# The first DFT stage of a long convolution: mirrored rows, one 8 KB run per row, order by hand

## The chip, the cores and the metric

The kernel runs on one core of a Trainium2 chip. The metric is the device time in microseconds (us). Three runs of the kernel before took 1265.47, 1269.49 and 1283.69 us, with a median of 1269.49.

A core has TensorE (PE), which multiplies a stationary operand (loaded first; the profile lists the weight load as PEld) with a moving one into PSUM, VectorE (DVE), ScalarE (ACT) and GpSimd (POOL), which work element by element, and SyncE (SP), which here only issues DMAs. DMAs are issued from SP's and ACT's queues and run on 16 DMA engines. Each engine works through its own instructions in order and waits for others by semaphores.

## What is computed

Inputs are x and v of 4 batches × 12800 positions × 128 channels, and a filter that comes from a small network.

```python
h_mlp = np.maximum(pos_emb @ w1, 0.0) @ w2
h_filt = h_mlp * np.exp(-0.01 * pos)[:, None]
u = x * v
y = causal_convolution(u, h_filt)        # by FFT of length 2 * 12800 in the reference
x1 = x * y
gate = sigmoid(sum_k conv_w[k] * x1 shifted by 4 - k positions)    # 5 taps
out = (gate * (x1 @ w_val)) @ w_out
```

All of it is float32. The gate's weights are 200 times larger than drawn, so small errors in x1 show in the output.

## The kernel before, in words

The 12800 positions are two halves (j) of 6400 = 100 × 64; a position is j·6400 + n1·64 + n2 with n1 below 100 and n2 below 64. The convolution is done in the frequency domain by a two-step DFT with odd frequencies 4·k1 + 1, which needs cosine and sine parts only.

**First stage** (span 0 to about 404 us). Partitions are n1. `chunks` lists 64 chunks, each one j and two n2. `fetch` loads x and v of a chunk for all four batches, `prep` multiplies them on DVE (u_t, line 257), and splits the product in a rounded part u_hi (ACT, line 258) and a rest u_lo (POOL, line 259), because the matmul is done in the fast float32r form. In `signal` each of four pieces (two batches, cosine or sine, 512 columns) is the sum of three matmuls: rounded table × u_hi, table's rest × u_hi, rounded table × u_lo (line 282). PSUM is copied by ACT (cosine, line 285) and DVE (sine, line 287) into st, and two DMAs store st into the DRAM tensor a_u, the cosine's on ACT's queue and the sine's on SP's. `_Split` (line 102) issues every such DMA as two, rows 0 to 95 and rows 96 to 99.

Beside it `filt` computes the filter's spectrum: transposes of pos_emb (tp, posT), the network's first layer (gp, g_sb), the 100-point DFT of the 64 hidden columns (ap, copied into ag), and then, for each k1, a 64-point DFT with a table fk that ACT and DVE build (lines 232 and 233) and PE applies (line 235). `signal` and `filt` are generators; a list of costs interleaves their steps, and a scheduler orders the recorded instructions by a timeline. Three weights come as 64-bit words and are narrowed on DVE by `_narrow`, at the ninth chunk.

**Second stage** (about 404 to 860 us). Fifty pairs of k1: a pair's rows of a_u are loaded (128 partitions of 4 KB, line 359), transformed over n2 (z_ps, line 341), multiplied with the filter's spectrum on DVE, combined on POOL, transformed back (c_ps, line 369, whose two row halves of 64 are two row tiles of the array), copied by ACT (line 376), and stored in c_y by ACT's queue in runs of 2 KB. The order is written by hand.

**Third stage** (about 860 us to the end). Rows of c_y (4 KB onto 100 partitions) and of x are loaded, the last 100-point transform, the product with x, the five taps, the gate and the two projections follow.

Buffers: the pool `ld` has six buffers of 128 × 2048 floats, which all stages share; u_t, u_hi, u_lo have two, st three.

## Time and profile before

| | |
|---|---|
| median of three runs | 1269.49 us |
| span of the profiled execution | 1273.6 us (its own time is not listed apart; the span stands for it) |
| PE, DVE busy over the span | 1144.7 us (90%), 1018.0 us (80%) |
| POOL, ACT busy over the span | 862.4 us (68%), 628.3 us (49%) |
| DMA over the span | 332.95 MB, 261 GB/s on average |
| first stage | last store issued at 403.7 us, first read of a_u at 408.2 us |

Busy times are those of one profiled execution. A group's row gives its source line, engine, operation, what it writes and reads, the shape and the count; then the busy time in us, the mean of one in ns, and the engine's idle time just before these instructions with what ended it. DMA share is the mean busy share of the 16 DMA engines. Shares over the whole span mix three stages with different limits, so the first stage has to be read by itself.

### The profile page before, as it was taken

To read this page: it belongs to the slowest core of one execution; us is meant where nothing else is said; L and a number is where in the kernel's file an instruction comes from. 1 tells how busy PE (TensorE), PEld (TensorE's weight loads), DVE (VectorE), ACT (ScalarE), POOL (GpSimd) and SP (SyncE) were. 2 spreads that over 40 slices of the span, in tenths; PEclk is the share of its full clock that TensorE was granted. 3 is DMA by queue.
4 is the path that set the end of the run, shared out by engine and by line. 5 is a ranking of instruction groups with operands and counts; after the bars stand their busy time and mean duration, and the time that the engine had idled before them with its cause. 6 is when DMAs were issued, how large, how long until landed. Compare 5 with 4: busy or idle time off the path is not lost. (4 is left out here: it accounts for less than half of the span.)

```text
span 1273.6 us, 16726 instructions
## 1 busy us (share of the span) xinstructions
PE 1144.7 (90%) x5500; PEld 570.2 (45%) x5500; DVE 1018.0 (80%) x1130; ACT 628.3 (49%) x1064; POOL 862.4 (68%) x346
## 2 busy tenths in 40 slices
PE   4878999978867889999999999988899999999986
PEld 3657776656544223333333333334344444444432
DVE  5956233797744999999999999951999999999997
ACT  3334454677633223333333333323576677667663
POOL 3334233434543669999999999962788988987980
PEclk9979899989977999999999999988999999999999
DMA  9999778889996667777787778539999989999942
GB/s 240 304 306 302 231 231 268 269 250 299 297 303 220 260 231 261 269 278 281 283 296 276 277 275 297 215 132 264 247 286 283 290 264 286 286 272 281 291 150 103
DMA packets 152255, 332.95 MB, mean 261 GB/s; under 512 B 12447, under 2 KB 64715, under 8 KB 150635
## 3 DMA queue, kind: packets, MB, share of 16 engines
q1 hardware_dynamic: 104256, 226.13, 58.8%
q10 hardware_dynamic: 47914, 105.76, 22.9%
q8 instruction: 45, 0.74, 0.2%
q14 instruction: 40, 0.32, 0.1%
HBM read 200.77 MB, written 131.07 MB: 261 GB/s over the span
## 5 line engine op out<-in xcount | busy, mean ns | idle before, releaser
L530 POOL TENSOR_TENSOR ext<-yr,xr 128x400 f32<-128x400 f32 x120 | 298.1, 2486 | 48.9 <-DVE yr L528 46.5
L259 POOL TENSOR_TENSOR u_lo<-u_t,u_hi 100x1024 fp32r<-100x1024 f32 x64 | 159.0, 2488 | 241.3 <-ACT u_hi L258 223.0
L545 DVE SCALAR_TENSOR_TENSOR gt<-ext,cw,gt 128x1600 f32<-128x1600 f32 x128 | 242.6, 1895 | 1.8 <-ACT gt L542 1.8
L376 ACT COPY c_sb<-c_ps 128x1024 f32<-128x1024 f32 x100 | 101.4, 1014 | 279.2 <-PE c_ps L369 279.2
L341 PE MATMUL z_ps<-ld 128*64 128x512 f32 x800 | 194.7, 606 | 7.9 <-DMA ld<-a_u 6.8
L428 POOL TENSOR_TENSOR va<-va,vb 128x1024 f32<-128x1024 f32 x50 | 156.4, 3127 | 36.6 <-DVE vb L346 36.5
L282 PE MATMUL fp<-u_hi,fwd_hi 100*100 100x512 f32 x256 | 118.7, 464 | 55.8 <-ACT st L285 21.8
L287 DVE COPY st<-fp 100x512 f32<-100x512 f32 x128 | 85.2, 685 | 74.2 <-PE fp L282 58.2
L503 PE MATMUL sd<-ld,inv 100*64 100x512 f32 x512 | 129.8, 611 | 10.6 <-DMA ld<-c_y 9.1
L346 DVE TENSOR_TENSOR vb<-z_ps,h_sb 128x2048 f32<-128x2048 f32 x50 | 114.5, 2289 | 23.8 <-ACT c_sb L376 23.6
L429 POOL TENSOR_TENSOR vc<-vc,vd 128x1024 f32<-128x1024 f32 x50 | 118.3, 2365 | 21.8 <-DVE vd L346 17.1
L564 PE MATMUL o_ps<-gd,wout 128*128 128x400 f32 x256 | 112.0, 519 | 18.3 <-DVE gd L559 10.7
L257 DVE TENSOR_TENSOR u_t<-ld 100x1024 f32<-100x1024 f32 x64 | 87.4, 1366 | 50.8 <-POOL u_lo L259 42.0
L346 DVE TENSOR_TENSOR va<-z_ps,h_sb 128x2048 f32<-128x2048 f32 x50 | 114.0, 2280 | 11.3 <-PE z_ps L341 11.3
L510 ACT COPY sd_sb<-sd 128x512 f32<-128x512 f32 x128 | 76.2, 596 | 90.4 <-PE sd L503 66.9
L430 POOL TENSOR_TENSOR va<-va,vb 128x1024 f32<-128x1024 f32 x50 | 118.4, 2368 | 0.0
L369 PE MATMUL c_ps<-vc,ld 64*128 64x512 f32 x400 | 100.7, 622 | 14.6 <-DVE vc L419 14.5
L282 PE MATMUL fp<-u_hi,fwd_lo 100*100 100x512 f32 x256 | 110.7, 432 | 0.0
L285 ACT COPY st<-fp 100x512 f32<-100x512 f32 x128 | 71.1, 594 | 76.0 <-PE fp L282 46.7
L554 PE MATMUL v_ps<-ext,wval 128*128 128x400 f32 x256 | 107.1, 500 | 0.0
L341 PEld LDWEIGHTS z_ps<-ld 128*64 128x64 f32 x800 | 54.4, 138 | 113.3 <-issue 85.6
L258 ACT CAST u_hi<-u_t 100x1024 fp32r<-100x1024 f32 x64 | 68.2, 1067 | 73.1 <-PE fp L282 40.9
(78 smaller groups left out, 1951.4 us busy)
## 6 DMA issues: line engine op xcount, KB each, us to landing
c_y<-c_sb ACTq DMA_DIRECT2D x100, 512.0 KB
ld<-a_u SPq DMA_DIRECT2D x49, 1024.0 KB
ld<-c_y SPq DMA_DIRECT2D x128, 384.0 KB
xr<-in_xt_dram SPq DMA_DIRECT2D x32, 800.0 KB
out_dram<-o_sb ACTq DMA_DIRECT2D x32, 800.0 KB
ld<-in_x_dram SPq DMA_DIRECT2D x64, 384.0 KB
ld<-in_v_dram SPq DMA_DIRECT2D x64, 384.0 KB
a_u<-st ACTq DMA_DIRECT2D x64, 384.0 KB
```

Of the source, the lines that this page charges most:

```text
L259: nc.gpsimd.tensor_tensor(lo, u_t, hi.bitcast(F32), op=ALU.subtract)
L282: nc.tensor.matmul(out=fp, lhsT=w[:, c], rhs=d[:, b:b + 2], start=(k == 0), stop=(k == 2))
L341: nc.tensor.matmul(out=z[half[h]], lhsT=wk[:, h, half[c]], rhs=a2[:, h, j], start=True, stop=True)
L346: nc.vector.tensor_tensor(out, z.rearrange("p (b d) -> p b d", d=D).unsqueeze(1).to_broadcast([128, n, B, D]), h_sb.unsqueeze(2).to_broadc ...
L428: nc.gpsimd.tensor_tensor(va[:, 0:2], va[:, 0:2], vb[:, 0:2], op=ALU.add)
L429: nc.gpsimd.tensor_tensor(vc, vc, vd, op=ALU.add)
L430: nc.gpsimd.tensor_tensor(va[:, 2:4], va[:, 2:4], vb[:, 2:4], op=ALU.add)
L503: nc.tensor.matmul(out=sd[c * N2:(c + 1) * N2], lhsT=inv[:, c], rhs=ct[c][:, r * B * D:(r + 1) * B * D], start=True, stop=True)
L530: nc.gpsimd.tensor_tensor(e[:, r0 + r], yr, xr, op=ALU.mult)
L545: nc.vector.scalar_tensor_tensor(gt, rows(t, k), cw[:, k:k + 1], gt, op0=ALU.mult, op1=ALU.add)
L554: nc.tensor.matmul(out=v_ps, lhsT=wval, rhs=rows(t)[:, r * ROW:(r + 1) * ROW], start=True, stop=True)
L564: nc.tensor.matmul(out=o_ps, lhsT=wout, rhs=gd, start=True, stop=True)
```

## The change

The transform over n1 is taken about the middle of the 100 rows, half a sample off. Row q and its mirror image 99 − q then have cosines that are equal and sines that are opposite, so the sum and the difference of the two rows carry everything, and 50 rows are contracted instead of 100.

- The host lays x and v out anew: for each n2 one row per (half of the batches h, pair q), with x and v, both j, the row and its mirror, two batches and 128 channels side by side: 2048 floats, 8 KB. The hundred rows (h, q) stand on partitions 14 to 113, so that h = 0 ends at partition 63 and h = 1 starts at 64.
- The 64 chunks are now the 64 values of n2, each with both j. `product` multiplies x and v on DVE (line 278). `folded` makes sums and differences on POOL, two instructions of 512 columns (line 286). `spectra` applies two tables (cos + sin to the sums, cos − sin to the differences) in full float32: per table two matmuls, one per h, on partitions 0 to 63 and 64 to 127 (line 296). The split into rounded part and rest is gone. The copies to st have 1024 columns each (lines 299 and 301).
- `store` writes a row's 2048 floats as one run; a_u is [k1, n2, 2, j, b, d] now. All of it goes by SP's queue. The second stage's table is recomputed for the two new parts, and its load takes them in the order (n2, part).
- Five of the six `ld` buffers hold chunks in rotation, fetched five ahead; the sixth holds pos_emb in two halves. The unused partitions of the five are cleared by ten memsets at the start (lines 313 and 314). u has two buffers, f three, st four.
- `filt` does the same work in a pipelined order (a step's matmuls are issued with the next step), g_sb is stored with n2 innermost, and the steps return their own cost; the loop over n2 is under a manual schedule. `_narrow` stands after n2 = 40, 46 and 52.

```diff
-        def prep(i):
-            x_t, v_t = ahead.pop(0)
-            u_t = p1.tile([N1, B, P1C * D], F32, name="u_t", bufs=2)
-            hi = p1.tile([N1, B, P1C * D], F32R, name="u_hi", bufs=2)
-            lo = p1.tile([N1, B, P1C * D], F32R, name="u_lo", bufs=2)
-            nc.vector.tensor_tensor(u_t, x_t, v_t, op=ALU.mult)
-            nc.scalar.copy(out=hi, in_=u_t)
-            nc.gpsimd.tensor_tensor(lo, u_t, hi.bitcast(F32), op=ALU.subtract)
-            return hi, lo
...
-                for b in range(0, B, 2):
-                    for c in range(2):
-                        fp = ps1.tile([N1, 2, P1C, D], F32, name="fp", bufs=4)
-                        for k, (w, d) in enumerate(((fwd_hi, hi), (fwd_lo, hi), (fwd_hi, lo))):
-                            nc.tensor.matmul(out=fp, lhsT=w[:, c], rhs=d[:, b:b + 2], start=(k == 0), stop=(k == 2))
...
+        def fetch(n):
+            t = held[n % XB]
+            sync_s.dma_start(out=t[P0:P0 + N1], in_=xv[n].rearrange("h q w j l b d -> (h q) (w j l b d)"))
+            return t.rearrange("p (w e) -> p w e", w=2)
+
+        def product(n):
+            t = fetched.pop(n)
+            u = p1.tile([128, J, 2, XE], F32, name="u", bufs=2)
+            nc.vector.tensor_tensor(
+                u.rearrange("p j l e -> p (j l e)"), t[:, 0], t[:, 1], op=ALU.mult)
+            us[n] = u
+
+        def folded(n):
+            u = us.pop(n)
+            f = p1.tile([128, 2, J, XE], F32, name="f", bufs=3)
+            for c, op in ((0, ALU.add), (1, ALU.subtract)):
+                nc.gpsimd.tensor_tensor(f[:, c], u[:, :, 0], u[:, :, 1], op=op)
+            folds[n] = f
+
+        def spectra(n):
+            f = folds.pop(n)
+            st = p1.tile([128, 2, J, B, D], F32, name="st", bufs=4)
+            for c in range(2):
+                fp = ps1.tile([128, 2, J, XE], F32, name="fp", bufs=2)
+                for h in range(2):
+                    r = slice(h * NH, (h + 1) * NH)
+                    nc.tensor.matmul(out=fp[:, h], lhsT=fold[r, c], rhs=f[r, c], start=True, stop=True)
+                o = st[:, c].rearrange("k j (h b) d -> k h j (b d)", h=2)
+                if c == 0:
+                    nc.scalar.copy(out=o, in_=fp)
+                else:
+                    nc.vector.tensor_copy(out=o, in_=fp)
+            done[n] = st
+
+        def store(n):
+            st = done.pop(n).rearrange("k c j b d -> k (c j b d)")
+            dst = a_u[:, n].rearrange("k c j b d -> k (c j b d)")
+            sync_s.dma_start(out=dst, in_=st[P0:P0 + N1])
+
+        fetched, us, folds, done = {}, {}, {}, {}
+        AHEAD1 = 5
+        with tc.manual_schedule():
+            for t in held:
+                nc.vector.memset(t[0:32], 0.0)
+                nc.vector.memset(t[96:128], 0.0)
+            fetched[0] = fetch(0)
+            fil = filt()
+            n_fil, spent = 16 * 1.3 + 0.7 + 16 * 0.9 + 16 * 1.5 + 25 * 1.9 + 0.5, 0.0
+            for n in range(1, AHEAD1):
+                fetched[n] = fetch(n)
+            product(0)
+            folded(0)
+            product(1)
+            for n in range(N2):
+                if n + AHEAD1 < N2:
+                    fetched[n + AHEAD1] = fetch(n + AHEAD1)
+                if n + 1 < N2:
+                    folded(n + 1)
+                if n + 2 < N2:
+                    product(n + 2)
+                spectra(n)
+                while spent < n_fil * (n + 1) / (N2 - 2):
+                    step = next(fil, None)
...
+                if n:
+                    store(n - 1)
+                if n == 40:
                     _narrow(nc, p1, wval, w_val)
+                if n == 46:
                     _narrow(nc, p1, wout, w_out)
+                if n == 52:
                     _narrow(nc, p1, cw, conv_w.rearrange("k d -> d k"))
...
-                    in_=a_u[2 * p + i:2 * p + i + step].rearrange("k c n j b d -> (c n) k (j b d)"))
+                    in_=a_u[2 * p + i:2 * p + i + step].rearrange("k n c j b d -> (n c) k (j b d)"))
```

Where the instructions moved stands in the prediction, at the two places it rests on: DMA issues on SP in the middle of the stage, and DVE where the tables fk are built. Names there: a_u and st are the spectra on their way to DRAM, ld a chunk of x and v, in_x, in_v and in_xv the inputs before and after, u_t and u the products, fk the filter's tables, raw, top and tmp the words of `_narrow`.

More of the change, by code (lines that the diff above doesn't have):

```diff
@@ L27 @@
 KG = 8
-P1C = 2
+NF, NH = N1 // 2, 64
+P0 = NH - NF
 R = 4
@@ L60, in _tables @@
     win = np.transpose(win, (1, 0, 2))
-    tabs = {"fwd": fwd, "inv": inv, "w": w, "dft": dft, "tw": tw, "win": win, "ident": np.eye(128)}
+    tabs = {"fwd": fwd, "fold": fold, "inv": inv, "w": w, "dft": dft, "tw": tw, "win": win, "ident": np.eye(128)}
     return {k: np.ascontiguousarray(a, dtype=np.float32) for k, a in tabs.items()}
@@ L148, in tile_longconv_gate @@
     cw = const.tile([D, KC], F32, name="cw")
+    nc.scalar.dma_start(out=fold, in_=t_fold)
     nc.scalar.dma_start(out=fwd, in_=t_fwd)
@@ L164, in load @@
         return ld.tile([128, 2048], F32, name="ld")
-    def split(src, name):
-        hi = const.tile(list(src.shape), F32R, name=name + "_hi")
-        lo = const.tile(list(src.shape), F32R, name=name + "_lo")
-        nc.vector.tensor_copy(out=hi, in_=src)
-        nc.vector.tensor_tensor(lo, src, hi.bitcast(F32), op=ALU.subtract)
-        return hi, lo
-    fwd_hi, fwd_lo = split(fwd, "fwd")
     ag_pool = tc.tile_pool(name="ag", bufs=1)
@@ L232, in filt @@
                     nc.scalar.activation(fk[:, i], dft[:, 1], AF.Copy, scale=tw[:, 1, k1:k1 + 1])
+                for i in range(4):
+                    k1 = k0 + i
                     nc.vector.scalar_tensor_tensor(
                         fk[:, i], dft[:, 0], tw[:, 0, k1:k1 + 1], fk[:, i], op0=ALU.mult, op1=ALU.add)
-                    nc.tensor.matmul(
-                        out=gz[:, i], lhsT=ag[:, k1].rearrange("p j e -> p (j e)"), rhs=fk[:, i], start=True, stop=True)
-                nc.scalar.copy(out=ag[:, k0:k0 + 4].rearrange("p k j e -> p k (j e)"), in_=gz)
@@ L238, in filt @@
-                yield
-        xv = x.rearrange("b (j a n) d -> j a b n d", j=J, a=N1)
-        vv = v.rearrange("b (j a n) d -> j a b n d", j=J, a=N1)
-        chunks = [(j, n0) for j in range(J) for n0 in range(0, N2, P1C)]
-        def fetch(i):
-            j, n0 = chunks[i]
-            ns = slice(n0, n0 + P1C)
-            t = load()[:N1].rearrange("a (w b e) -> a w b e", w=2, b=B)
-            for w, src in enumerate((xv, vv)):
-                sync_s.dma_start(out=t[:, w], in_=src[j][:, :, ns].rearrange("a b n d -> a b (n d)"))
-            return t[:, 0], t[:, 1]
@@ L264, in signal, with after @@
-        def signal():
-            ready = [prep(0)]
-            for i, (j, n0) in enumerate(chunks):
-                if i == 8:
+                if after:
+                    after()
+                def after(k0=k0, fk=fk):
+                    gz = ps1.tile([128, 4, 2 * N2], F32, name="gp", bufs=1)
+                    for i in range(4):
+                        nc.tensor.matmul(
+                            out=gz[:, i], lhsT=ag[:, k0 + i].rearrange("p j e -> p (j e)"), rhs=fk[:, i],
+                            start=True, stop=True)
+                    nc.scalar.copy(out=ag[:, k0:k0 + 4].rearrange("p k j e -> p k (j e)"), in_=gz)
@@ L289, in signal @@
-                for c in range(2):
-                    (scalar_s if c == 0 else sync_s).dma_start(
-                        out=a_u[:, c, ns, j].rearrange("k n b d -> k n (b d)"),
-                        in_=st[:, c].rearrange("k n b d -> k n (b d)"))
-        FS = 0.9
-        sig, fil = signal(), filt()
-        n_sig = len(chunks) * B // 2
-        cost = [0.7, 0.9] * (J * N2 // 8) + [0.8] * (FO // 4) + [1.6] * (FO // 4) + [0.9] * (N1 // 4)
-        spent, steps = 0.0, iter(cost)
-        for i in range(n_sig):
-            next(sig, None)
-            while spent < sum(cost) and spent * n_sig * FS <= (i + 1) * sum(cost):
-                next(fil, None)
-                spent += next(steps, sum(cost))
@@ L305, in tile_longconv_gate @@
-        for _ in sig:
-            pass
-        for _ in fil:
-            pass
+            for _ in fil:
+                pass
+            store(N2 - 1)
     with tc.tile_pool(name="p2", bufs=1) as p2, tc.tile_pool(name="ps2", bufs=1, space=PSUM) as ps2:
```

101 lines of the change are left out of this document (59 added, 42 removed).

## The prediction

> **What bounds the kernel now.** The kernel has three stages, and the change touches the first alone. I began with the busy time by stretch of the span, to see where the first stage ends and what is full in it. The columns are the stretch, its length, then busy us (and instructions) of PE, PE weight load, DVE, ACT and POOL, the granted clock, the mean share of the 16 DMA engines and GB/s.
>
> ```profile
> core 0: us, PE busy (x) PEld busy (x) DVE busy (x) ACT busy (x) POOL busy (x), PEclk, DMA share, GB/s
> 0.00:404.00 404.00, 333.51 (x1930) 244.39 (x1932) 246.15 (x367) 202.93 (x350) 159.21 (x68) 0.92 0.89 271
> 20.00:120.00 100.00, 80.90 (x454) 60.48 (x454) 77.56 (x124) 34.79 (x50) 36.96 (x15) 0.93 0.99 302
> 120.00:400.00 280.00, 243.93 (x1453) 178.50 (x1454) 159.68 (x230) 161.24 (x288) 116.20 (x47) 0.90 0.86 264
> 410.00:420.00 10.00, 7.30 (x27) 3.41 (x28) 5.03 (x3) 1.14 (x3) 0.40 (x1) 0.74 1.01 393
> 500.00:600.00 100.00, 100.00 (x476) 34.34 (x474) 93.43 (x60) 37.53 (x59) 93.92 (x36) 1.00 0.79 279
> 860.00:900.00 40.00, 32.29 (x144) 15.18 (x142) 13.31 (x29) 15.13 (x33) 14.67 (x12) 0.91 1.00 268
> ```
>
> Two things are nearly full in the first 404 us: PE at 333.5 us (83%) and the DMA engines at 0.89. The stage moves 404 × 271 = 109.5 MB. Dividing GB/s by share gives what the DMA engines would move at full share: 302/0.99 = 305 and 264/0.86 = 307 in this stage, 279/0.79 = 353 in the second, 268 at the start of the third, and 393/1.01 = 389 while the second stage fetches its first rows. So with PE taken away altogether the stage would still need 109.5/306 = 358 us of DMA.
>
> Next the groups of instructions of the stage, the list of waits from 20 to 400 us, and the handover to the second stage on the timeline.
>
> ```profile
> L282 PE MATMUL fp<-u_hi,fwd_hi 100*100 100x512 f32 x256 | 118.7, 464 | 55.8 <-ACT st L285 21.8 <-ACT u_hi L258 20.2 <-DVE st L287 12.6
> L257 DVE TENSOR_TENSOR u_t<-ld 100x1024 f32<-100x1024 f32 x64 | 87.4, 1366 | 50.8 <-POOL u_lo L259 42.0 <-DMA ld<-in_x_dram 3.1 <-DMA a_u<-st 2.8
> L287 DVE COPY st<-fp 100x512 f32<-100x512 f32 x128 | 85.2, 685 | 74.2 <-PE fp L282 58.2 <-DMA a_u<-st 15.9
> L258 ACT CAST u_hi<-u_t 100x1024 fp32r<-100x1024 f32 x64 | 68.2, 1067 | 73.1 <-PE fp L282 40.9 <-DVE u_t L257 9.2 <-DMA a_u<-st 7.5
> L259 POOL TENSOR_TENSOR u_lo<-u_t,u_hi 100x1024 fp32r<-100x1024 f32 x64 | 159.0, 2488 | 241.3 <-ACT u_hi L258 223.0 <-PE gp L235 18.2
> L233 DVE SCALAR_TENSOR_TENSOR fk<-dft,tw,fk 128x128 f32<-128x128 f32 x100 | 51.6, 565 | 10.8 <-ACT fk L232 10.7
> DVE st L287 <- PE fp L282: 58.0, 44, 4.9
> ACT st L285 <- PE fp L282: 44.5, 30, 5.3
> ACT st L285 <- DMA a_u<-st: 18.5, 8, 5.6
> 403.70 1.47 SPq L102 DMA_DIRECT2D a_u<-st  x2
> 408.22 2.36 SPq L359 DMA_DIRECT2D ld<-a_u  x5
> 411.73 1.09 PE L341 MATMUL z_ps<-ld 128*64 128x512 f32 x1 [6.83 <-DMA ld<-a_u]
> ```
>
> DVE and ACT wait for PE (58 and 44.5 us), and PE in turn for them: the engines hand a chunk round in a ring, and the 11% of idle DMA comes from it. The stage ends when the last store has landed (issue at 403.7, first read at 408.2), and the second stage starts 8 us behind the last store's issue. That handover stays as it is, so what the stage gains or loses the kernel gains or loses.
>
> **The change part by part: TensorE.** The three split matmuls per chunk, 768 in all, go, and 256 of 64 rows by 512 columns in two row tiles come. The second stage has the same form; the first row is the busy time of the old matmuls alone in the stage.
>
> ```profile
> 0.00:404.00 404.00, 226.17 (x768) 133.02 (x768) 0.92 0.89 271
> L369 PE MATMUL c_ps<-vc,ld 64*128 64x512 f32 x400 | 100.7, 622 | 14.6 <-DVE vc L419 14.5
> L376 ACT COPY c_sb<-c_ps 128x1024 f32<-128x1024 f32 x100 | 101.4, 1014 | 279.2 <-PE c_ps L369 279.2
> ```
>
> They cost 100.7/400 = 0.252 us apiece, so 64 us in place of 226 us, and PE falls from 333 to about 171 us. If the two row tiles do not overlap, the bound is 256 × 0.622 = 159 us and 266 us in all, still far below the DMA time. PE stops being a bound either way.
>
> **ACT, DVE and POOL.** ACT loses the cast (68 us) and copies 64 times 1024 elements at 1.014 us (65 us for 71). DVE keeps its 64 products at 1.37 us and its copies (64 × 2 × 0.685 = 88 us at most). POOL trades 64 subtractions of 1024 elements for 128 sums and differences of 512. No row has POOL at 512, so the bounds are half of 2.488 us and all of it. I take half, 1.24, since its rows of 1024 scale with the elements, and POOL stays near 159 us. New on DVE are ten memsets of 32x2048 at the very start. The sizes nearest to them stand at the start of the timeline, with the first fetch of now and the wait for the first table:
>
> ```profile
> 0.83 0.17 DVE L151 MEMSET w1bd<- 128x128 f32 x1 [0.83 <-PEq L645]
> 1.00 0.27 DVE L152 MEMSET w2bd<- 128x256 f32 x1
> 0.74 0.88 SPq L102 DMA_DIRECT2D ld<-in_x_dram  x2
> 4.45 0.32 DVE L169 CAST fwd_hi<-fwd 100x300 fp32r<-100x300 f32 x1 [3.18 <-DMA fwd<-in_tab_fwd_dram]
> ```
>
> 128 columns more cost 0.10 us, so 2048 columns cost 0.27 + 14 × 0.10 = 1.67 us and ten cost 17 us. Each fetch waits for the two memsets of its buffer. The first leaves at about 4.6 us where now it leaves at 0.74, the fifth at 18, and the sixth waits for the first product at 19. Five fetches are 4.1 MB, 12 us of transfer, so the DMA engines lose about 6 us there. DVE as a whole comes to 246 + 17 = 263 us, so it does not bound the stage as a total.
>
> **The transfers** are the term that decides. The bytes stay, to 0.1 MB, but a row's run becomes 8 KB each way. Here are DMA issues on SP in the middle of the stage, before the change (ld is the chunk's x and v, st its spectra; the bracket names what an issue waits for).
>
> ```order
> L102 DMA a_u_63<-st_2375 96x2x512 [waits DMAHW7_49,DVE_49]
> L102 DMA a_u_63<-st_2375 4x2x512 [waits DMAHW0_49]
> L102 DMA ld_2847<-in_x_dram 96x4x256 [waits DMAHW1_49,DVE_49]
> L102 DMA ld_2847<-in_x_dram 4x4x256 [waits DMAHW2_49]
> L102 DMA ld_2847<-in_v_dram 96x4x256 [waits DMAHW3_49]
> ```
>
> The same queue after the change:
>
> ```order
> L113 DMA a_u_63<-st_1567 96x2048 [waits DMAHW2_49,DVE_49,Activation_49]
> L113 DMA a_u_63<-st_1567 4x2048 [waits DMAHW3_49]
> L113 DMA ld_101<-in_xv_dram 96x2048 [waits DMAHW4_49]
> L113 DMA ld_101<-in_xv_dram 4x2048 [waits DMAHW5_49]
> L113 DMA a_u_63<-st_1600 96x2048 [waits DMAHW6_49,DVE_49,Activation_49]
> L113 DMA a_u_63<-st_1600 4x2048 [waits DMAHW7_49]
> ```
>
> A load row was four runs of 1 KB (256 floats) and a store row two of 2 KB; both are now one of 8 KB (2048 floats). All stores moved onto SP, ahead of the next fetch, where half of them were ACT's. With eight semaphores in turn and two issues per transfer, about four transfers of 0.82 MB are in flight, so a store that waits for its copies holds up the fetch behind it, but three transfers (7 us) cover that.
>
> No row shows 8 KB on 100 partitions in both directions. Above stand 389 (4 KB reads onto 128 partitions) and 353 (4 KB reads with 2 KB writes, 128 partitions); below stand 306 (this stage, short runs, 100 partitions) and 268 (the third stage's 4 KB reads onto 100 partitions, with its x rows). The partitions and the mix of reads and writes are those of 306, the run length points to 353, and I take the middle, 330: 109.5/330 = 332 us. [...]
>
> **What is late next.** In the last part of the stage DVE's order changes. Here it stands at the tables fk, before the change (u_t and u are products, st copies of the spectra).
>
> ```order
> L233 SCALAR_TENSOR_TENSOR fk<-dft,tw,fk 128x128 x3
> L287 COPY st<-fp 100x2x2x128
> L233 SCALAR_TENSOR_TENSOR fk<-dft,tw,fk 128x128 x5
> L257 TENSOR_TENSOR u_t<-ld 100x1024
> L287 COPY st<-fp 100x2x2x128 x2
> ```
>
> And after it, at the second of the three weights that are narrowed there:
>
> ```order
> L278 TENSOR_TENSOR u<-ld 128x1024
> L301 COPY st<-fp 128x2x2x256
> L252 SCALAR_TENSOR_TENSOR fk<-dft,tw,fk 128x128 x4
> L86 TENSOR_SCALAR top<-raw 128x128
> L87 TENSOR_SCALAR tmp<-raw 128x128
> L88 TENSOR_TENSOR top<-top,tmp 128x128
> ```
>
> The narrowing moved from the stage's beginning into the fk stretch, between four fk and the next chunk's product, which follows its last row. Its first instruction waits for a load issued just ahead of it; the only row of such a wait is the 3.2 us for the table fwd. With some dozen small instructions behind it I charge 5 us for each of the three, 15 us, between nothing (the transfers in flight cover it) and 25. At the end the last chunk's product, fold, matmuls and copy (1.2 + 2.5 + 1.0 + 1.4 us) leave the DMA engines half idle: 5 us.
>
> The sum: 332 + 6 + 15 + 5 = 358 us where 404 stood, 46 us less. The profiled span is 1273.6 us, so 1227.6, and since it is 4.1 us over the median of the runs (1269.49), the forecast is 1223.5 us.
>
> **The rivals.** *Full speed transfers* (0.15): at 353 the stage takes 310 + 26 = 336 us, 68 less, and the time is 1201.5. At 389 it would be 1173, but DVE's 263 us and the waits round it keep it from going so low; I stop at 320 us, 1185. For it speaks the one run per row, against it the 100 partitions.
>
> *Run length is worth nothing* (0.17): 306 stays, 358 + 26 = 384, 20 less, 1249.5. For it: the quotient is the same, 305 and 307, in a full and in a less full stretch, so it looks like a property of the traffic.
>
> *DVE and POOL shut each other out* (0.10):
>
> ```profile
> L257 DVE TENSOR_TENSOR u_t<-ld x64: 1208/1216/3415, 7.9 to 394.8; 100x1024 f32<-100x1024 f32 x64
> L233 DVE SCALAR_TENSOR_TENSOR fk<-dft,tw,fk x100: 334/341/2546, 15.6 to 333.1; 128x128 f32<-128x128 f32 x100
> L287 DVE COPY st<-fp x128: 673/684/702, 23.1 to 403.0; 100x512 f32<-100x512 f32 x128
> ```
>
> Minimum, median, maximum: products and fk are at times longer by one POOL subtraction (2.2 us of 2.5), copies from PSUM never. In the fk stretch (25 steps over 28 chunks) a chunk has 2.5 us on POOL, 1.2 for the product and 0.9 × 4 × 0.34 = 1.2 for fk, which exclude each other: 4.9 us, just the DMA time of a chunk (1.64 MB / 330 = 5.0). If each chunk also waits out one POOL instruction (1.24), it adds 28 × 1.2 = 34 us: 392, 12 less, 1257.5.
>
> *The four odd rows pace the queue* (0.06): every transfer is split into 96 and 4 rows. If four of the 16 engines always had 7 rows against a mean of 6.25, the transfers would take 332 × 7/6.25 = 372, the stage 398, and the time 1263.5. Against it: with the same split the mean share reached 0.99, where four pacing engines allow 0.89. [...]
>
> *100 partitions throttle long runs* (0.07), the slower side: at 268, the third stage's price, the transfers take 409, the stage 435, 31 more, and the time is 1300.5. It is slower from below 109.5/(404 − 26) = 290, and by over 2% below 272. For it: that row is the only one with long reads onto 100 partitions. Against it: there nearly all packets are reads, here half.
>
> **How the numbers follow.** The forecast keeps 0.45; its own range, with 318 to 345 GB/s and 8 to 22 us for the narrowing, is 1201 to 1242. Two per cent, about what can be told from no change, is 1244 and 1295. Below 1244 lie the forecast (0.43), full speed (0.15), a third of the 306 case (0.06) and a little of the DVE case (0.02): 0.66. Above 1295 lies most of the last rival, 0.06; 0.28 remains. The range 1188 to 1262 leaves out that rival, half of the odd-row case and the ends of the first.
>
> **What would show it.** The stage's last store at about 358 us with GB/s over share near 330 confirms the main term; a share well under 0.9 in the middle would say that an engine bounds it instead. PE busy near 171 us, POOL's fold near 1.24 us, the first product at 19 us, and DVE idle at the three narrowings test the rest. Wrong would be a quotient at 306 or below, or an fk stretch over 5.5 us per chunk.

## The result and the profile after

The changed kernel takes 1253.76 us (median; 1249.01 to 1274.54) where the kernel before, run beside it, takes 1269.53 us (1255.66 to 1285.80). The ratio is 0.9925 with a 95% interval of 0.9899 to 0.9951: faster by 0.5 to 1.0%, less than the 2% that was named as the bound. The forecast was 1223.5 us, and only about a third of the expected 46 us has come. The time lies inside the range 1188 to 1262, but the range reached to within 8 us of the time before; a time below 1244 had been given 0.66, one within 2% of the time before, as it came, 0.28.

The busy time by stretch of the first stage (columns as in the prediction: stretch, length, PE, PE weight load, DVE, ACT, POOL, granted clock, DMA share, GB/s) shows where it stays:

```profile
core 0: us, PE busy (x) PEld busy (x) DVE busy (x) ACT busy (x) POOL busy (x), PEclk, DMA share, GB/s
0.00:389.00 389.00, 260.18 (x1672) 142.98 (x1672) 251.78 (x311) 133.24 (x222) 166.25 (x132) 0.86 0.88 281
0.00:60.00 60.00, 26.23 (x136) 15.66 (x136) 44.06 (x41) 7.36 (x7) 21.07 (x20) 0.94 0.81 222
60.00:260.00 200.00, 149.08 (x1208) 87.10 (x1208) 107.20 (x116) 70.98 (x102) 90.12 (x71) 0.86 0.97 314
260.00:360.00 100.00, 62.52 (x234) 30.05 (x234) 74.14 (x122) 39.42 (x85) 39.88 (x30) 0.75 0.78 249
360.00:389.00 29.00, 22.35 (x97) 10.16 (x96) 26.38 (x34) 15.49 (x31) 15.19 (x12) 1.00 0.83 288
```

The stage moves 389 × 281 = 109.3 MB, as before. In its middle no engine is near full, and the DMA share is 0.97 with 314 GB/s; at the start and in the fk stretch the share is lower and so is the rate. Price the lost bytes at 314 GB/s. From 0 to 60 us 13.3 MB are moved, worth 42 us, so 18 are lost. From 260 to 360 us 24.9 MB, worth 79: 21 lost. From 360 on 8.4 MB, worth 27: 2 lost. With 109.3 / 314 = 348 us for the bytes that makes 389.

The groups of instructions of the stage (line, engine, operation, shapes, count, then busy us, mean ns, then idle time before them with what ended it):

```profile
L296 PE MATMUL fp<-f,fold 64*128 64x512 f32 x512 | 160.3, 738 | 101.9 <-POOL f L286 47.6 <-ACT st L299 43.1 <-DVE st L301 10.9
L286 POOL TENSOR_TENSOR f<-u 128x512 f32<-128x512 f32 x128 | 166.1, 1320 | 219.1 <-DVE u L278 198.5 <-PE ap L239 9.7 <-PE fp L296 5.8
L278 DVE TENSOR_TENSOR u<-ld 128x1024 f32<-128x1024 f32 x64 | 80.6, 1261 | 47.3 <-DMA ld<-in_xv_dram 44.7 <-POOL f L286 2.4
L299 ACT COPY st<-fp 128x1024 f32<-128x1024 f32 x64 | 64.8, 1012 | 211.5 <-PE fp L296 110.2 <-DMA a_u<-st 97.1 <-PE gp L260 3.7
L313 DVE MEMSET ld<- 32x2048 f32 x5 | 8.8, 1765 | 2.3 <-issue 2.3
L86 DVE TENSOR_SCALAR top<-raw 128x128 int32<-128x128 int32 (+1 forms) x3 | 0.6, 209 | 34.1 <-DMA raw<-in_moe_w_val_dram 16.6 <-DMA raw<-in_moe_conv_w_dram 9.4 <-DMA raw<-in_moe_w_out_dram 8.1
```

DVE waits 44.7 us for loads before its products, and ACT 97.1 us for a store to free the tile of spectra: both ends of the pipe wait for transfers, which the kernel before did not show to this degree (18.5 us for ACT's copy, 3.1 us for the product). The last row is the second loss: DVE stands 34.1 us before the first instruction of the three narrowings. The timeline shows the end of the memsets with the first product, the narrowing's first wait, and the handover to the second stage:

```profile
19.52 1.76 DVE L313 MEMSET ld<- 32x2048 f32 x1 [0.48 <-issue]
21.75 1.76 DVE L314 MEMSET ld<- 32x2048 f32 x1 [0.47 <-issue]
23.54 2.36 DVE L278 TENSOR_TENSOR u<-ld 128x1024 f32<-128x1024 f32 x2
...
259.24 0.33 ACTq L80 DMA_DIRECT2D raw<-in_moe_w_val_dram  x1
259.74 1.01 ACT L299 COPY st<-fp 128x1024 f32<-128x1024 f32 x1 [9.36 <-DMA a_u<-st]
267.37 0.23 DVE L86 TENSOR_SCALAR top<-raw 128x128 int32<-128x128 int32 x1 [16.65 <-DMA raw<-in_moe_w_val_dram]
...
272.08 5.97 POOL L286 TENSOR_TENSOR f<-u 128x512 f32<-128x512 f32 x4 [22.30 <-DVE u L278]
...
389.23 0.68 SPq L113 DMA_DIRECT2D a_u<-st  x2
393.73 2.42 SPq L394 DMA_DIRECT2D ld<-a_u  x5
397.03 1.94 PE L376 MATMUL z_ps<-ld 128*64 128x512 f32 x2 [6.63 <-DMA ld<-a_u]
```

The last store is issued at 389.2 us (403.7 before, 358 forecast) and the second stage's first matmul of z_ps starts at 397.0 us (411.7 before): 14.7 us gained. This start, the first number behind the three durations in the row below, is the measure of the stage in all experiments, each read from one profiled execution; a time given without a ratio is that of a single run. The second number is the start of the last such matmul, the end of the second stage.

```profile
L376 PE MATMUL z_ps<-ld x800: 592/592/1116, 397.0 to 817.5; 128*64 128x512 f32 x160
```

### The profile page after: what moved, and what is told of

Its sections match the earlier page's. It is cut to its first block, busy times and chain, and to the rows that moved or that the text cites. A ratio compares the mean times of both kernels' runs of the same rounds, so it can differ in the third digit from the quotient of the medians.

```text
span 1251.4 us, 15855 instructions
## 1 busy us (share of the span) xinstructions
PE 1073.3 (86%) x5244; PEld 470.7 (38%) x5244; DVE 1014.8 (81%) x1074; ACT 558.7 (45%) x936; POOL 874.0 (70%) x410
## 5 line engine op out<-in xcount | busy, mean ns | idle before, releaser
L286 POOL TENSOR_TENSOR f<-u 128x512 f32<-128x512 f32 x128 | 166.1, 1320 | 219.1 <-DVE u L278 198.5
L296 PE MATMUL fp<-f,fold 64*128 64x512 f32 x512 | 160.3, 738 | 101.9 <-POOL f L286 47.6
L463 POOL TENSOR_TENSOR va<-va,vb 128x1024 f32<-128x1024 f32 x50 | 159.5, 3190 | 38.8 <-DVE vb L381 19.5
L299 ACT COPY st<-fp 128x1024 f32<-128x1024 f32 x64 | 64.8, 1012 | 211.5 <-PE fp L296 110.2
L381 DVE TENSOR_TENSOR vb<-z_ps,h_sb 128x2048 f32<-128x2048 f32 x50 | 114.6, 2291 | 25.2 <-ACT c_sb L411 24.9
L599 PE MATMUL o_ps<-gd,wout 128*128 128x400 f32 x256 | 112.3, 520 | 17.9 <-DVE gd L594 10.4
L381 DVE TENSOR_TENSOR va<-z_ps,h_sb 128x2048 f32<-128x2048 f32 x50 | 114.1, 2282 | 11.6 <-PE z_ps L376 11.1
L278 DVE TENSOR_TENSOR u<-ld 128x1024 f32<-128x1024 f32 x64 | 80.6, 1261 | 47.3 <-DMA ld<-in_xv_dram 44.7
L465 POOL TENSOR_TENSOR va<-va,vb 128x1024 f32<-128x1024 f32 x50 | 118.6, 2371 | 0.0
L296 PEld LDWEIGHTS fp<-f,fold 64*128 64x128 f32 x512 | 53.2, 217 | 159.2 <-POOL f L286 81.9
L301 DVE COPY st<-fp 128x1024 f32<-128x1024 f32 x64 | 78.1, 1220 | 31.7 <-DMA a_u<-st 20.4
L404 PE MATMUL c_ps<-va,ld 64*128 64x512 f32 x400 | 99.4, 615 | 0.1
```

The costliest lines, as they stand in the source:

```text
L286: nc.gpsimd.tensor_tensor(f[:, c], u[:, :, 0], u[:, :, 1], op=op)
L296: nc.tensor.matmul(out=fp[:, h], lhsT=fold[r, c], rhs=f[r, c], start=True, stop=True)
L381: nc.vector.tensor_tensor(out, z.rearrange("p (b d) -> p b d", d=D).unsqueeze(1).to_broadcast([128, n, B, D]), h_sb.unsqueeze(2).to_broadc ...
L404: nc.tensor.matmul(out=c_ps[:, h], lhsT=wk[half[h], 2 + c], rhs=vt[half[h], c].rearrange("p b d -> p (b d)"), start=(c == 0), stop=(c == 1))
L463: nc.gpsimd.tensor_tensor(va[:, 0:2], va[:, 0:2], vb[:, 0:2], op=ALU.add)
L465: nc.gpsimd.tensor_tensor(va[:, 2:4], va[:, 2:4], vb[:, 2:4], op=ALU.add)
```

## The experiments

**Where the time of the changed kernel stays.** Theory A: DVE's waits for the weights hold the stage up from 260 us on, and the memsets at its start. Theory B: the transfers set the pace anyway, and what DVE gains they take back. The first edit issues the three raw loads at the kernel's start, into buffers of their own; the arithmetic of the narrowing stays where it was.

```diff
-def _narrow(nc, pool, dst, src):
+def _narrow(nc, pool, dst, raw):
-    raw = pool.tile([p, n], mybir.dt.int64, name="raw")
-    nc.scalar.dma_start(out=raw, in_=src)
...
+    for i, (dst, w) in enumerate(((wval, w_val), (wout, w_out), (cw, conv_w.rearrange("k d -> d k")))):
+        raw = const.tile(list(dst.shape), mybir.dt.int64, name=f"raw{i}")
+        nc.scalar.dma_start(out=raw, in_=w)
```

> The three loads of the 64-bit weights are issued at the start, into buffers of their own; the narrowing stays after n2 = 40, 46 and 52. Theory A (the waits for these loads, 16.6 + 8.1 + 9.4 us of DVE, drain the transfers in flight and set the pace from 250 to 360 us): the first matmul of the second stage moves from 397 us to 375 to 382, the DMA share from 260 to 360 us rises from 0.78 to over 0.9, and the time is 1232 to 1240. Theory B (the transfers need that time anyway, so the waits are hidden): 397 stays within 4 us and the time within 0.4% of 1254.

Measured: 1243.84 us, ratio 0.9845 (0.9721 to 0.9968). Its stretch from 260 to 360 us and its row of z_ps:

```profile
260.00:360.00 100.00, 75.02 (x308) 38.95 (x308) 79.45 (x136) 48.03 (x108) 47.20 (x39) 0.82 0.97 307
L379 PE MATMUL z_ps<-ld x800: 592/592/1114, 378.3 to 810.9; 128*64 128x512 f32 x160
```

The fk stretch goes from 249 to 307 GB/s and the second stage starts 18.7 us earlier, close to the 21 us read off the windows. So the waits for the three weights cost some 19 us of this stage.

The second edit gives five of the ten memsets to POOL.

```diff
-                nc.vector.memset(t[96:128], 0.0)
+                nc.gpsimd.memset(t[96:128], 0.0)
```

> Five of the ten memsets at the start go to POOL, so that the two of a buffer run side by side. Theory A (the memsets hold back the fetches, which leave 4.5 us apart instead of 2.5): first product at 13 to 15 us instead of 23.5, the first matmul of the second stage 7 to 10 us earlier than 397, time 1244 to 1247. Theory B (the later stalls of the stage absorb whatever the start gains): the first product is earlier but the second stage starts within 3 us of 397.

Measured: 1248.98 us, ratio 0.9887 (0.9774 to 1.0001); the first product starts at 11.9 instead of 23.5 us, and z_ps at 389.7 us, 7.3 us earlier. Of 11.6 us at the start, 7.3 reach the stage's end.

Both edits together, with the narrowing's arithmetic placed earlier (after chunks 16, 20 and 24):

> Both edits, and the narrowing moved to n2 = 16, 20 and 24, where DVE has only the product and a copy per row. Theory A: the gains add, second stage from 362 to 372 us, time 1218 to 1230, the share over 0.93 from 40 to 350 us. Theory B (transfers bound the stage): not below 385 us and not below 1240.

Measured: 1242.75 us, ratio 0.9839 (0.9724 to 0.9955). Two stretches, the first of loads alone, and z_ps:

```profile
4.00:14.00 10.00, 0.00 (x0) 0.00 (x0) 7.92 (x5) 0.00 (x0) 6.30 (x5) 1.00 1.01 228
60.00:260.00 200.00, 148.90 (x1224) 86.43 (x1224) 121.52 (x158) 72.17 (x103) 92.09 (x74) 0.89 0.98 314
L379 PE MATMUL z_ps<-ld x800: 592/592/1116, 377.5 to 810.1; 128*64 128x512 f32 x160
```

The gains do not add: 377.5 us, hardly below the first edit's 378.3. That is neither theory A's 362 to 372 us nor theory B's 385 or more, but that the gains do not add speaks for the transfers as the bound once DVE's waits are gone, as theory B has it. And the first row has a surprise: with nothing but loads under way (x and v, and small tables on ACT's queue), the DMA engines are at a share of 1.01 and yet move only 228 GB/s. The next runs ask what limits them; all but the first are this kernel with one more edit, unless something else is said.

**Is it an engine after all?** The filter's work in this stage is left out of the changed kernel:

> The filter's whole work in the first stage is left out (pos_emb, its transposes, first layer, 100-point DFT, tables fk); ag is cleared once on POOL at the start. It shows what the signal path alone needs. If the transfers run at 330 GB/s wherever no engine disturbs them, 106 MB take 321 us and the second stage starts at 350 to 362 us. If the rate in the changed kernel is held down by the traffic itself (316 GB/s on average over the stage), it starts no earlier than 370.

Measured: 1234.47 us, z_ps at 369.3 us, 27.7 us earlier, next to the second theory's 370. Two stretches (the middle 200 us ran at 299 GB/s):

```profile
0.00:60.00 60.00, 22.78 (x76) 7.28 (x78) 50.64 (x32) 10.39 (x10) 46.12 (x26) 0.99 0.91 283
40.00:60.00 20.00, 12.21 (x44) 3.67 (x46) 18.88 (x12) 5.06 (x5) 20.00 (x12) 0.97 1.01 382
```

Though PE's work falls from 149 to 109 us in the middle 200 us, the rate there does not rise (299 GB/s for 314), so the filter's instructions do not hold the transfers up in that stretch. At the start the filter's work does cost: 283 GB/s here for 222. The run cannot settle more, since the filter's bytes are gone (106 MB for 109.5, some 11 us at 314 GB/s) and the waits for the weights were still in this kernel (17.5 + 16.5 + 12.7 us). But it shows 382 GB/s for 20 us with the four odd rows split off every transfer.

**The length of the runs.** Loads go back to 1 KB runs, the order of x and v in memory being changed to suit:

```diff
+                out=t[P0:P0 + N1].rearrange("p (s e) -> p s e", s=8),
+                in_=xv[n].rearrange("w j l h q b d -> (h q) (w j l) (b d)"))
```

> On top of the kernel with both edits (weights loaded early, memsets split), the host lays x and v out in eight pieces, so that a load row is eight runs of 1 KB again; stores keep 8 KB. If run length is worth what the prediction took (306 to 330 GB/s for loads and stores together), the loads' half costs 11 to 24 us and the second stage starts at 388 to 402 us instead of 377.5. If the partitions set the loads' rate whatever the run length, it starts within 4 us of 377.5.

Measured: 1257.72 us, ratio 0.9961 (0.9914 to 1.0009), z_ps at 392.2 us, 14.7 us later. So the long run of the loads, together with the order in memory that goes with it, is worth some 15 us of the stage.

**The queue.** All stores are issued by ACT:

```diff
-            sync_s.dma_start(out=dst, in_=st[P0:P0 + N1])
+            scalar_s.dma_start(out=dst, in_=st[P0:P0 + N1])
```

> On top of both edits all stores are issued by ACT instead of SP. If the order on SP (a store that waits for its copies ahead of the next fetch, four transfers in flight) costs DMA time, the share from 60 to 360 us rises from 0.97 and the second stage starts 5 to 12 us earlier than 377.5. If the transfers are the bound, it stays within 4 us, or is later where ACT now waits for DVE's copy before it can issue.

Measured: 1230.34 us, z_ps at 355.0 us, 22.5 us earlier, more than either theory gave.

**The four odd rows.** A transfer of 100 rows is split in 96 and four. Here the loads of the last four are left out:

```diff
-            sync_s.dma_start(out=t[P0:P0 + N1], in_=xv[n].rearrange("h q w j l b d -> (h q) (w j l b d)"))
+            nc.sync.dma_start(out=t[P0:P0 + 96], in_=xv[n].rearrange("h q w j l b d -> (h q) (w j l b d)")[0:96])
```

> On top of both edits the loads of the last four of the 100 rows are left out (these rows stay zero); stores keep all rows. By bytes (2.1 of 109.5 MB) the second stage starts 6 to 8 us earlier than 377.5. If the four engines that take these rows pace the queue, a row's pair of transfers falls from 14 to 13 packets on them, 7%, and it starts 22 to 26 us earlier, at 351 to 356.

Measured: 1194.06 us, and

```profile
60.00:260.00 200.00, 157.75 (x1306) 91.62 (x1304) 142.34 (x192) 88.74 (x139) 108.78 (x85) 0.93 1.00 350
L379 PE MATMUL z_ps<-ld x800: 592/592/1116, 335.2 to 755.6; 128*64 128x512 f32 x160
```

Leaving out 2% of the bytes takes 42.3 us off the stage, six times what the bytes cost and nearly twice the pacing theory's own estimate. It also makes one DMA of two per load. The same edit was then made alone on both original kernels. On the changed one:

> The changed kernel itself, nothing else altered, with the last four of the 100 rows left out of its loads (the loads onto 96 rows stay, 64 transfers of four rows go; rows 160 to 163 of the tile keep their zeros, so four of the 100 rows are left out of what is computed). Its first z_ps stood at 397.0 us. Theory that the four odd rows pace the queue: the stretches 60:200, which ran at 315 to 325 GB/s, go to about 350, and the start moves by much of the 42 us that the same edit was worth with the early raw loads; the three waits of DVE for the weights (34 us) stay and hide some of it, so 362 to 376 us. Rival, that only the bytes count: 2.1 MB less at 281 to 325 GB/s is 6 to 8 us, 389 to 391 us. Rival, that the waits for the weights hide it: 385 to 397 us.

```profile
L376 PE MATMUL z_ps<-ld x800: 592/592/1114, 366.7 to 795.2; 128*64 128x512 f32 x160
```

It starts z_ps 30.3 us earlier (time 1230.23 us), with 22.7 us of waits for the weights still there. On the kernel before:

> The kernel before with the last four of the 100 rows left out of its loads of x and v (128 transfers of 16 KB go; product, halves and the contraction run over 96 rows, so four rows are left out of what is computed; the tile shapes are otherwise unchanged and the stores keep their odd rows). Its first z_ps stood at 411.7 us. Theory that the odd rows paced this queue too: its share was 0.97 to 1.01 from 20 to 120 us and 0.89 to 0.90 from 200 to 360, so in these 260 us a gain of about a tenth, 20 to 26 us: first z_ps at 385 to 392 us. Rival, that PE with three matmuls for one (77.1 of 80 us busy from 120 to 200) and the short runs of 1 KB bound it and the four rows cost their bytes: 2.1 MB at 270 GB/s is 8 us, 402 to 405 us, or nothing, 409 to 414 us.

```profile
60.00:260.00 200.00, 187.12 (x1268) 138.28 (x1268) 102.69 (x140) 95.04 (x133) 74.81 (x31) 0.94 0.88 263
L341 PE MATMUL z_ps<-ld x800: 592/592/1116, 406.9 to 841.7; 128*64 128x512 f32 x160
```

There it brings 4.8 us (time 1275.77 us), the price of the bytes at most, and the rate does not rise (263 GB/s, 270 with the rows). So the four rows cost no more than their bytes in the kernel before and 30 us after the change. That the ring of engines hid them before, and that the change ran into them by taking PE out of the way, is argued, not shown: the change also moved all stores, with their four-row transfers, onto SP's queue, and the run with the stores on ACT shows that the queue matters while the four rows are there.

**Keep the rows, fill the transfer.** The loads are padded with zero rows to 128, in one transfer each; the memsets go:

```diff
-            sync_s.dma_start(out=t[P0:P0 + N1], in_=xv[n].rearrange("h q w j l b d -> (h q) (w j l b d)"))
+            nc.sync.dma_start(out=t, in_=xv[n].rearrange("h q w j l b d -> (h q) (w j l b d)"))
...
-                nc.vector.memset(t[0:32], 0.0)
-                nc.gpsimd.memset(t[96:128], 0.0)
...
+    padded = np.zeros((N2, 2, NH) + rows.shape[3:], rows.dtype)
+    padded[:, 0, P0:], padded[:, 1, :NF] = rows[:, 0], rows[:, 1]
```

> On top of the early loads of the weights the host pads each load to 128 rows (28 rows of zeros), one DMA in place of two, and all memsets go. Loads bring 14.7 MB more. If a transfer onto 100 partitions is slow because it fills some of the ways into the memory more than others (loads alone run at 228 GB/s at a share of 1.01 there, 393 at 1.01 onto 128 partitions), the padding is nearly free: the quotient in the first 20 us is over 320 and the second stage starts at 365 to 385 us. If bytes count, 14.7 MB at 320 are 46 us and it starts at 405 to 423 less 8 us for the memsets.

Measured: 1214.1 us, ratio 0.9663 (0.9513 to 0.9812), and

```profile
4.00:14.00 10.00, 3.79 (x8) 1.14 (x8) 4.78 (x4) 0.00 (x0) 5.40 (x4) 1.00 1.02 400
L376 PE MATMUL z_ps<-ld x800: 592/592/1114, 356.8 to 777.3; 128*64 128x512 f32 x160
```

Loads alone run at 400 GB/s where 96 and four rows ran at 228, at about the same share. With 14.7 MB more to move the stage is 20.7 us shorter. Three things changed at once here: the rows, the four-row transfers of the loads and the memsets.

The stores are padded as well (a_u gets 128 rows, and the second stage reads the middle 100), first on SP, then on ACT:

```diff
-    a_u = dram.tile([N1, N2, 2, J, B, D], F32, name="a_u")
+    a_u = dram.tile([128, N2, 2, J, B, D], F32, name="a_u")
...
-            sync_s.dma_start(out=dst, in_=st[P0:P0 + N1])
+            nc.sync.dma_start(out=dst, in_=st)
```

> The kernel with loads onto 128 rows (its first z_ps at 356.8 us), and now the stores too in one transfer of all 128 rows each, on SP as before: a_u has 128 rows, of which the second stage reads the middle 100; 14.7 MB more written, no transfer of four rows left in the stage. Theory that transfers of four rows pace the queue: start earlier, 325 to 345 us. Rival, that the bytes count: 14.7 MB at the 382 GB/s of its 60:260 stretch is 38 us, 390 to 396 us. If neither holds and both cancel: 350 to 365 us.

> The same with all stores issued by ACT. Theory that a load waits behind a store on SP's one queue (moving the stores to ACT was worth 22.5 us with the loads on 96 and four rows): first z_ps 10 to 22 us earlier than with the padded stores on SP, whole time 1170 to 1205 us. Rival, that those 22.5 us came from the four-row transfers sharing a queue with the loads and are gone with them: within 5 us of the padded stores on SP. POOL's 165 us, DVE's 217 to 252 and PE's 254 us of work in this stage leave room down to about 290 us.

Measured: z_ps at 353.6 us on SP (1211.65 us), 349.3 us on ACT; the latter takes 1206.86 us, ratio 0.9568 (0.9462 to 0.9675). Its stretch:

```profile
60.00:260.00 200.00, 146.88 (x1249) 85.56 (x1249) 124.87 (x175) 82.17 (x128) 99.62 (x80) 0.93 1.01 423
```

On SP the third case came, that both cancel: the rate rises to 422 GB/s and pays for the 14.7 MB, no more. And without transfers of four rows, the change of queue is worth 4.3 us, not 22.5, as the rival has it. These two kernels differ from the earlier pair in the padding too and already run at 422 GB/s on one queue, so that the 22.5 us hung on the four-row transfers is likely, not shown.

**Even share, or all 128 partitions?** The first two runs take 112 rows, of which an even share would be seven for each of sixteen engines, and the unpadded 100 rows, in one transfer each way:

```diff
-            sync_s.dma_start(out=t[P0:P0 + N1], in_=xv[n].rearrange("h q w j l b d -> (h q) (w j l b d)"))
+            nc.sync.dma_start(out=t[8:120], in_=xv[n].rearrange("h q w j l b d -> (h q) (w j l b d)"))
...
-            sync_s.dma_start(out=dst, in_=st[P0:P0 + N1])
+            nc.scalar.dma_start(out=dst, in_=st[8:120])
```

> Loads and stores of 112 rows in one transfer each (rows 8 to 119 of the tile: six rows of zeros, the 100, six of zeros), stores on ACT; the tile's other rows are cleared by the memsets on DVE and POOL as with the raw loads early. 16.8 MB less than with 128 rows both ways (first z_ps 349.3 us, 423 GB/s from 60 to 260 us). Theory that an even share of the 16 engines is what counts: the rate stays at 400 to 425 GB/s, 16.8 MB / 423 GB/s = 40 us less of transfers, first z_ps at 309 to 328 us (the DMA share may fall below 0.95 where DVE, PE or POOL become late). Rival, that only transfers over all 128 partitions reach that rate: 122 MB at 310 to 350 GB/s and a start of 6 us, 355 to 400 us.

> The 100 rows of a load and of a store in one transfer each, neither padded nor split in 96 and four; stores on ACT, raw loads early, memsets on both engines. Theory that a transfer's rows are dealt out in equal numbers to as many engines as divide them (10 for 100 rows): the stage's DMA share is at most 0.63 and the rate about 10/16 of the 423 GB/s that 128 rows reached, 264 GB/s: 109.5 MB in 415 us, first z_ps at 415 to 440 us. Rival, that the small transfers of four rows were the whole cost and 100 rows go to all 16 engines: share above 0.9 and first z_ps at 300 to 355 us. [...]

The 100 rows in one piece take 1318.74 us:

```profile
60.00:260.00 200.00, 126.81 (x1106) 74.53 (x1107) 90.24 (x115) 55.08 (x64) 72.81 (x59) 0.83 0.65 261
L379 PE MATMUL z_ps<-ld x800: 592/592/1114, 445.3 to 881.8; 128*64 128x512 f32 x160
```

A share of 0.65 and 261 GB/s, 0.62 of the 423 that 128 rows reached. As an estimate from these figures, 0.65 × 16 is the packet time of 10.4 engines, and 261 GB/s the bytes of 9.9 at the 26.4 GB/s (423/16) that each had with 128 rows. That fits the ten of the first theory; how rows are dealt out to the engines no run shows.

The 112 rows give a time of 1207.14 us, ratio 0.9519 (0.9391 to 0.9647), no better than 128 rows, and the start of z_ps was neither theory's. That left the loads open: in kernels with 96 and four, 96, or 112 rows they run at 228 to 242 GB/s when alone, but these kernels also have memsets beside them, which the padded ones have not. Three more runs part these: the memsets put back beside 128 rows; 112 rows for the stores only; and 112 rows both ways once more.

> Loads and stores of 128 rows in one transfer each, stores on ACT (first z_ps at 349.3 us; loads alone from 4 to 14 us at 400 GB/s, 60:260 at 423), and ahead of the first loads the ten memsets of 32 rows again, five on DVE and five on POOL, of no use to the result. Theory that 128 rows make the early rate: from 4 to 14 us still 340 GB/s or more at a share near 1, and first z_ps later only by the start lost, 3 to 10 us. Rival, that the memsets beside the loads slow them (the only other difference of that stretch): 228 to 260 GB/s there. For the stretch 60:260, in which no memset runs, both give 415 to 425.

> Loads of 128 rows, stores of 112 rows (seven for each of 16 engines), each in one transfer, stores on ACT, no memsets. 7.3 MB less than with 128 rows both ways (first z_ps 349.3 us, 423 GB/s from 60 to 260 us). Theory that an even share counts: the rate stays at 415 to 425 GB/s and z_ps starts 14 to 20 us earlier, at 329 to 335 us. Rival, that a transfer's rate goes with the partitions it covers (bytes of padding are then nearly free): rate 395 to 412 GB/s, z_ps at 343 to 352 us, whole time within 0.6% of the kernel with 128 rows both ways.

> 112 rows both ways as before, on the same chip as the two others. Its profile showed 386 GB/s from 60 to 260 us and z_ps at 344.5 us in one of its longer executions. Theory that an even share counts: in an undisturbed execution 405 to 425 GB/s and z_ps at 309 to 330 us. Rival, that the rate goes with the partitions covered: 375 to 395 GB/s and 338 to 350 us again.

Loads alone from 4 to 14 us: first 96 rows (the kernel without odd rows in its loads), then 128 rows beside memsets, then 112 rows:

```profile
4.00:14.00 10.00, 0.00 (x0) 0.00 (x0) 7.92 (x5) 1.28 (x1) 6.30 (x5) 1.00 1.02 238
```

```profile
4.00:14.00 10.00, 0.00 (x0) 0.00 (x0) 8.87 (x6) 1.28 (x1) 6.30 (x5) 1.00 0.97 347
```

```profile
4.00:14.00 10.00, 0.00 (x0) 0.00 (x0) 7.92 (x5) 1.28 (x1) 6.30 (x5) 1.00 0.99 242
60.00:260.00 200.00, 152.52 (x1272) 89.78 (x1272) 131.87 (x180) 82.81 (x126) 101.65 (x80) 0.91 1.01 384
L379 PE MATMUL z_ps<-ld x800: 592/592/1115, 346.1 to 774.7; 128*64 128x512 f32 x160
```

So loads of all 128 rows are the fast ones; the memsets take the 400 to 347 at most (the first load also starts 2.8 us later there; z_ps starts at 353.4 us, 4.1 later, in 1211.68 us), and an even share without all partitions does nothing for loads alone. With 112 rows both ways the rival's figures came again, 384 GB/s and 346.1 us. Stores are otherwise. With loads of 128 rows and stores of 112:

```profile
60.00:260.00 200.00, 153.27 (x1306) 87.89 (x1302) 149.73 (x194) 93.22 (x149) 107.23 (x84) 0.97 1.01 423
L376 PE MATMUL z_ps<-ld x800: 592/592/1115, 333.5 to 770.1; 128*64 128x512 f32 x160
```

the rate stays at 423 GB/s and the stage is 15.8 us shorter than with 128 rows both ways, as the theory of the even share has it. In the whole time little of it is left: the last z_ps starts at 770.1 us, 771.1 with 128 rows both ways, and 1202.24 us is 0.4% under 1206.86, within the 0.6% of the rival. It is the lowest median of all kernels that compute everything, ratio 0.9497 (0.9440 to 0.9554), but its interval overlaps that of 128 rows both ways and that of 112 rows both ways on the same chip (1207.03 us, 0.9497 to 0.9604).

Why only loads of all 128 rows are fast when alone, no run shows; the cause in the expectation of the padded loads was the author's guess. If a load of 112 rows took no longer than one of 128, it would give 400 × 112/128 = 350 GB/s, an estimate from the 400 above; 242 were measured.

## Why the prediction was right or wrong

**The transfers: the rate was wrong.** The step "I take the middle, 330" put 332 us; the stage's middle ran at 314, which is 348 us for the same bytes, 16 too many. The method failed, not just the figure. It divided GB/s by share and took the quotient for what the engines can do. But the share counts the time that packets are under way, not what they carry: 1.01 goes with 228 GB/s on 96 and four rows, and 1.02 with 400 on 128. The packet records in the traces show the same: from 60 to 260 us an 8 KB packet had a median of 309 ns in all these kernels, at which pace sixteen engines make 424 GB/s, but a mean of 398 in the changed kernel, 369 without the loads' four rows and with the weights early, and 312 with loads of 128 rows and stores of 128 or 112. So the engines were busy with slower packets, and the quotient was no limit. And its bounds from rows with 100 partitions, 306 and 268, carried the split and the uncovered partitions within them, while the row of 389 GB/s, with 128, was the price of another layout, 4 KB reads without any split.

**The four odd rows: dismissed by an argument that does not hold.** That "with the same split the mean share reached 0.99, where four pacing engines allow 0.89" was the whole case against, and it got 0.06. The share stood at 0.97 to 0.98 in kernels that the four rows held back by 30 and 42 us: idle engines are one way to lose time, slower packets another. The rival pointed at the right transfers, but the mechanism that it named, four engines with more rows than the rest, accounts for a part at most: at 26 GB/s per engine (423/16), an engine with seven rows against a mean of 6.25 would allow 423 × 6.25/7 = 378 GB/s. Without the filter that was reached for 20 us (382), and 314 were measured in the middle. What the 128 four-row transfers cost beyond uneven numbers is not settled. That moving half of them to another queue gave 331 GB/s speaks for something in the queue; the split also makes two DMAs of one, with eight semaphores in turn, and no run parts that from the four rows. Another part of the gap goes with the loads' uncovered partitions (350 GB/s with loads of 96 rows, 382 with 128, the stores split in both). Which engines the four rows go to no run shows.

**100 partitions throttle long runs:** the rival's mechanism was there, its size was not. Loads alone were held to 228 to 242 GB/s, even below the 268 of its row, but mixed with stores the stage kept 281 on average and did not get slower.

**Run length is worth something,** so the rival that set it at nothing falls: 14.7 us for the loads. The quotient rose from 306 to 324 (314/0.97), but with 423 GB/s measured it is no limit.

**The start: mis-sized.** The memset was right (1.77 us for 1.67), but each is followed by some 0.47 us, so the ten took until 23.5 us instead of 19. The 6 us in "the DMA engines lose about 6 us there" became 18 for the first 60 us; half the memsets off DVE gave back 7.3. Part of the 18 is the filter's start, as the run without it shows (283 GB/s there for 222).

**The narrowing: right place, wrong size.** DVE idles at the three narrowings as foretold. The step "the only row of such a wait is the 3.2 us for the table fwd" was the trap: that load ran at the very start, these in the full stage, and 3.2 us became 16.6, 8.1 and 9.4. The first load took 8.1 us from its issue until DVE went on (259.24 to 267.37). The other half of its wait came before the issue: by the profile ACT, which issues it, had stood idle for 9.36 us until a store ended that. The row was not the only one either: the first narrowing of the kernel before waited 1.2 us, with other work of DVE between the load's issue and its use. The term of 15 us (up to 25) is 21 by lost bytes and 18.7 by experiment.

**The end** held better than charged: 2 us in place of 5. Together 16 + 12 + 6 − 3 = 31 us, which is 389 for 358.

**TensorE is no bound,** as said, but its price was wrong: 260 us busy instead of 171. The row taken for c_ps counts two records for each of the program's matmuls, as here (512 for 256), so one costs 0.50 us and not 0.25, and 256 of them 129 us by that row; 160.3 were measured, by chance the 159 that was given as the bound. That is 0.63 us for one in float32 (160.3/256), where the float32r form took 0.29 before (226.17/768), both of 512 columns.

**ACT, DVE, POOL:** POOL's fold has a median of 1.27 us (1.24 taken, half of the 2.49 for 1024 elements; that POOL scales so, no row of the kernel before showed), DVE comes to 252 us in the stage (263). DVE and POOL do shut each other out at times, as before: fk has a median of 0.341 us, but a mean of 0.608 and a maximum of 1.437, and all 35 of the 100 that took over 0.5 us ran mostly beside a fold of POOL and ended about 0.15 us behind its end. But it does not set the pace. The tile views give minimum, median and maximum, and the timeline a steady chunk:

```profile
L286 POOL TENSOR_TENSOR f<-u x128: 1257/1269/2273, 24.9 to 384.3; 128x512 f32<-128x512 f32 x128
L252 DVE SCALAR_TENSOR_TENSOR fk<-dft,tw,fk x100: 336/341/1437, 216.9 to 381.5; 128x128 f32<-128x128 f32 x100
287.64 1.21 DVE L278 TENSOR_TENSOR u<-ld 128x1024 f32<-128x1024 f32 x1
292.13 1.21 DVE L278 TENSOR_TENSOR u<-ld 128x1024 f32<-128x1024 f32 x1
```

A chunk takes 4.49 us there, when nothing is narrowed, under the 4.9 of that rival.

**The handover:** "what the stage gains or loses the kernel gains or loses" holds only to some 10 us in a single profile: of the 18.7, 7.3 and 19.5 us that the first three experiments gave the stage, 9.9, 4.8 and 11.0 came in the medians of the whole time. The second stage, from the first to the last z_ps, took 420.5 us in the changed kernel, 428.6 before, and 420 to 439 in the experiments without being edited but for its reading address. Its start is the part that varies: from 20 to 100 us behind its first z_ps TensorE was busy 80 us in the changed kernel, 72 in the kernel before and 68 with stores of 112 rows, and later on 98 to 100 us of every 100 in all three. Why was not tested.

## What to carry to other kernels

Before pricing a transfer, look at its rows: 100 rows in one transfer ran at 261 GB/s where 128 ran at 423, and leaving out a remainder of four rows, in a transfer of its own per load, made this stage 30 to 42 us shorter. Padding loads from 100 rows to 128 and stores to 112 costs bytes and still brought this kernel, with the weights loaded early and the stores on ACT, to 5% under the time before. A DMA share near one is no proof that the transfers are at their limit (1.01 went with 228 GB/s, 1.02 with 400); compare GB/s with the best rate of like transfers. When a bound is removed, ask first what was hidden behind it: the four rows cost 5 us before and 30 after. And a load whose wait is short at the very start (3.2 us for fwd before) should not be issued just ahead of its use in a full stage (16.6, 8.1 and 9.4 us here).

## What the runs showed of the hardware that was not expected

- The loads of x and v alone, 4 to 14 us: 228 GB/s with 96 and four rows, 238 with 96, 242 with 112, 347 to 400 with 128, all at shares of 0.97 to 1.02.
- Loads and stores together, 60 to 260 us: 261 GB/s (100 rows in one transfer, share 0.65), 314 (96 and four), 350 (loads of 96 rows only), 384 (112 both ways), 423 (loads of 128, stores of 112 or 128).
- Median time of a packet from 60 to 260 us, by the traces' packet records: 8 KB 309 ns (128 rows both ways), and in the kernel before 84 ns for 2 KB and 46 ns for 1 KB. That is 26.5, 24.4 and 22.3 GB/s per engine.
- A memset of 32x2048 on DVE repeats every 2.24 us, of which the profile lists 0.47 us as idle.
